# Spreading Q and dO into the padded tile on VectorE, and turning more middle units in pairs by DMA

## The chip, the cores and the metric

The kernel runs on one core of one Trainium2 chip. The metric is the device time of one execution in microseconds (us); the time shown for a kernel is the median of its runs.

## What is computed

The reference is forward and backward of a gated mix of two branches over 2048 tokens of width 512. Branch A is attention with 32 heads of 16 and a sliding causal window of 256 tokens, branch B a gated feed-forward layer of inner width 1376. The kernel returns the output and the gradients of x and of six weights.

```python
def _A_ref(x, wqkv, wo):
    ...
    scores = jnp.einsum("bhqd,bhkd->bhqk", q, k) * (Dh ** -0.5)
    mask = (idx[:, None] - idx[None, :] >= 0) & (idx[:, None] - idx[None, :] < W)
    p = _softmax(jnp.where(mask[None, None], scores, -1e9), axis=-1)
    ...
g = _sigmoid((x * gate_w).sum(-1, keepdims=True))
return g * _A_ref(x, wqkv, wo) + (1 - g) * _B_ref(x, W_gate, W_up, W_down)
...
_out, _vjp = jax.vjp(_f, A_x, A_wqkv, A_wo, B_W_gate, B_W_up, B_W_down, gate_w)
```

## The kernel before

There are three stages: feed-forward with its weight gradients (0 to about 248 us), attention forward and backward (to about 712 us), and the output with the gradient of x (to the end). The change lies in attention.

**Units.** Attention goes over 4 columns c of 8 heads (128 features), in each over 16 query blocks j of 128 tokens, and in each block over up to 3 key blocks kb and 2 halves (every second head, 4 heads). One (c, j, kb, half) is a unit; there are 360, listed at L646 to L660. The role of a unit is "d" (diagonal, kb = j), "m" (middle, kb = j - 1) or "f" (far, kb = j - 2). Half 1 of a block takes its units in the order m, d, f.

**One unit.** TensorE makes the scores ST (L671) and, from dO and V, dPT (L698). ScalarE takes the exponential of ST into Pu (L684). For "d" and "f" GpSimd masks it (L686, L689). VectorE multiplies it by dPT into Pd (`gradp`, L703). Three units later (LAG) TensorE uses Pu and Pd in the row sums BA (L712, L714); at a block's end ScalarE copies BA to SBUF (L718), and small operations on VectorE and GpSimd make from it the rows rq.

**PSUM.** ST, dPT, the projections (`pp`) and the gradient pieces (`wps`) share the tag M with 4 banks. A bank of ST is free after the exponential, one of dPT after `gradp`.

**Turning.** The gradients of K and V (CD, L533 and L536) need Pu and Pd transposed. `flip` (L723) has two ways. If `u.dma` is set, SyncE issues one transposing DMA (L731); with `u.pair` both halves of a block are turned by one DMA once half 1 is done, else half 0 alone. If it is not set, TensorE does 8 transposes of 128 x 128 (L741) into PSUM, and ScalarE and VectorE by turns copy them out (`evac`, L72 or L74). Before the change "d" units are pairs; "m" units of columns 0 to 2 are pairs for odd j, and for j = 4, 6, 8 in columns 1 and 2; in the other even blocks half 0 goes by DMA, from the tile PPs with one buffer, and half 1 over TensorE. Pairs of "m" lie in PPm with two buffers, pairs of "d" in PPd with three. Far units always go over TensorE.

**Groups and the padded tile.** Four blocks form a group gi = (c, tg) of 512 tokens; there are 16. During a group the planner projects the next one (`project_parts`, L118): Q, dO, a row transpose by DMA (`tr_rows`, L171), K, V, and K and V turned to rows (`tr_kv`). Q and dO land side by side in the tile zT (128 x 2 x 512). ST and dPT handle four heads at once, so they need Q and dO in a padded tile `zt`: four copies of the 512 columns of which copy k holds only partitions 32k to 32k + 31, with zeros elsewhere. `spread` (L512) fills part k. For the first group this is done by small copies in `mm` (L151); for the 15 others by four DMAs from SyncE.

**The order.** It is written by the loop at L877, one step per unit n. Operations planned for later stand in `ev` by step, with their engine's name: "pool" ones come ahead of `gradp`, "dve" ones behind it, "dma" ones at the end of the step. `credit` estimates TensorE's spare time and decides when a projection part (`prq`) or a gradient piece (`bgq`) is taken; a unit that turns over TensorE costs 0.44 (L934). When Q and dO of the next group have been projected (`len(prq) == 4`, L951), the four spreads and `flush` (stores that have gathered) are planned as "dma" at step n + 1; `tr_rows` is the next projection part. All DMAs named here, transposing or plain, are issued by SyncE in this order.

Of the kernel before, what the change touches and what calls it, by code (L numbers as in the profile page):

```python
# [22 lines left out]
def kernel(  # L23
# [20 lines left out]
    nc = tc.nc  # L44
# [11 lines left out]
    DC = D // P  # L56
# [48 lines left out]
    ZB = 2  # L105
    wq = ctx.enter_context(tc.tile_pool(name="wq", bufs=1))
    zt = [wq.tile([P, 2, NP, TPG, P], BF, tag=f"z{i}", name=f"z{i}") for i in range(ZB)]
# [4 lines left out]
    if True:  # L112
        HH = HG // 2
        proj = {}
        groups = [(c, tg) for c in range(DC) for tg in range(NTG)]
# [74 lines left out]
    with ExitStack() as p1, tc.manual_schedule():  # L190
# [148 lines left out]
        for fc in range(FC):  # L339
            for tg in range(NTG):  # L340
                k = Step()
# [97 lines left out]
        for n in range(N1 + 8):  # L439
# [35 lines left out]
            t = n - DA0  # L475
# [18 lines left out]
            z = n - DA0 - NT - 2  # L494
# [6 lines left out]
    if True:  # L501
# [9 lines left out]
        pools["now"] = (ps, "M", 4, psr, "TR")  # L511
        def spread(gi, k):  # L512
            rows = slice(32 * k, 32 * k + 32)
            nc.sync.dma_start(zt[gi % ZB][rows, :, k, :, :].rearrange("p w t q -> p w (t q)"),
                              proj[groups[gi]]["z"][rows, :, :])

        P2 = {}
        RQ = {}
# [128 lines left out]
        for c in range(DC):  # L647
            for j in range(NT):
                kbs = [k for k in (j - 1, j, j - 2) if k >= 0]
                for half in range(2):  # L650
                    order = kbs if half or len(kbs) < 3 else [kbs[0], kbs[2], kbs[1]]
                    for ki, kb in enumerate(order):
                        u = Unit()
                        u.c, u.j, u.kb, u.half = c, j, kb, half
                        u.first = ki == 0 and half == 0
                        u.last = ki == len(kbs) - 1 and half == 1
                        u.role = ("d", "m", "f")[j - kb]
                        u.pair = u.role == "d" or (u.role == "m" and c < DC - 1 and (j % 2 == 1 or (c > 0 and j in (4, 6, 8))))
                        u.dma = u.pair or (u.role == "m" and half == 0 and (c < DC - 1 or j < 10))
                        units.append(u)  # L660
        NU = len(units)
# [177 lines left out]
        with tc.manual_schedule():  # L839
            ev = {}  # L840
# [6 lines left out]
            n = 0  # L847
# [6 lines left out]
            def background():  # L854
                f, more = bgq.pop(0)
                store = f()
                if store is not None:
                    copies.append(store)
                    if len(copies) > 2 or gi + 2 >= len(groups):
                        ev.setdefault(n + 2, []).append(("dma", flush))  # L860
                return more
# [15 lines left out]
            while n <= NU + LAG or ev or cdq or bgq:  # L877
                now = ev.pop(n, [])
                u = units[n] if n < NU else None
                if u is not None:  # L880
                    gi = u.c * NTG + u.j // TPG
# [30 lines left out]
                w = units[n - LAG] if LAG <= n < NU + LAG else None  # L912
# [24 lines left out]
                if n >= NU:  # L937
                    if bgq:
                        held = background()
                    elif n > NU + 1:  # L940
                        for _ in range(2):
                            if len(S2["grads"]) > DC:
                                S2["grads"].pop(0)()
                elif held and credit > 0.3:
                    held = background()
                    credit -= 0.65
                elif prq and not held and ((credit > 0.4 and n > fed + 1) or due - n <= len(prq)):
                    fed = n
                    credit -= (0.44, 0.86, 0.86, 0.1, 0.86, 0.86)[len(prq) - 1]
                    prq.pop(0)()  # L950
                    if len(prq) == 4:  # L951
                        for k in range(NP):
                            ev.setdefault(n + 1, []).append(("dma", lambda gi=gi, k=k: spread(gi + 1, k)))
                        ev.setdefault(n + 1, []).append(("dma", flush))
                    if not prq:
                        late += plan.get(gi + 1, [])
                elif bgq and len(prq) <= 2 and credit > 0.3:
                    held = background()
                    credit -= 0.65
# [25 lines left out]
    with ExitStack() as p56:  # L985
        x_r5 = x_r

        with ExitStack() as p6:
# [20 lines left out]
            for g in range(NG):  # L1009
# [3 lines left out]
                for tl in range(GT):  # L1013
                    t = g * GT + tl
# [108 lines left out]
```

## Time and profile before

| | |
|---|---|
| median of 3 runs | 918.95 us (917.79 to 922.31) |
| profiled execution | 917.72 us, its span 916.0 us |
| p2m<-PPm, p2m<-PPs, p2d<-PPd: transposing DMAs (L731) | 36, 18, 62 |
| their median time from issue to landing (PPm, PPs, PPd) | 5.3, 4.4, 5.4 us |
| z<-zT (L514), plain DMAs of 64 KB | 60, 2.8 us to landing |
| TensorE transposes at L741 | 1184 (148 units of 8) |
| copies p2m<-pt: ScalarE, VectorE | 23 of 1.012 us, 13 of 0.683 us |
| `gradp` (L703), PPd, Pd, PPm | 682, 678, 671 ns each |

The profile is one execution on the chip. PE is TensorE, PEld its weight loads, DVE VectorE, ACT ScalarE, POOL GpSimd, SP SyncE; SPq is SyncE's queue of DMA issues. Tiles are named without numbers, so p2m<-PPm is a transpose of any PPm tile. In a timeline a row has the start, the duration, the engine, the line, the operation and the shapes; the bracket at the end tells how long the engine was idle before it and what released it. Matmuls are pipelined, so their durations overlap, and the distance between starts is what one costs. PEclk is the clock that TensorE was granted, in tenths of full speed.

### The profile page before, as it was taken

What the parts mean: (1) busy time and instruction counts of PE and PEld (TensorE: products, weight loads), DVE (VectorE), ACT (ScalarE), POOL (GpSimd) and SP (SyncE); (2) the same over time, 40 slices, a digit from 0 to 9 for tenths busy, and PEclk for the clock granted to TensorE, in tenths of its full rate; (3) what the DMA queues carried; (4) which work ended last, traced back from release to release, by engine and by line L of the source; (5) the groups of instructions that cost most, each with busy time, mean ns of one, the idle gap of its engine ahead of it and who ended that gap; (6) DMA issues with size and microseconds to landing.
All of it is one profiled execution on the core that took longest, in us unless ns stands there. A gap on an engine that the chain in (4) does not pass through costs nothing.

```text
span 916.0 us, 26488 instructions
## 1 busy us (share of the span) xinstructions
PE 899.1 (98%) x10757; PEld 576.2 (63%) x10863; DVE 486.2 (53%) x907; ACT 446.1 (49%) x782; POOL 486.5 (53%) x937
## 2 busy tenths in 40 slices
PE   8999999999999999999999999999999999999998
PEld 5556656556657777667676677777777644444445
DVE  4433344334277777657776677776677222322323
ACT  6422232222368777667776677776688200000111
POOL 4544545445276777767777577775677321111111
PEclk9999999999999999999999999999999999999999
DMA  9998879999699999998999989999999999777741
GB/s 300 194 200 188 192 179 216 221 219 200 159 167 160 170 158 164 178 177 169 178 172 184 186 163 179 179 169 171 186 155 191 251 237 254 183 184 185 184 92 47
DMA packets 490923, 168.07 MB, mean 183 GB/s; under 512 B 414960, under 2 KB 489680, under 8 KB 490800
## 3 DMA queue, kind: packets, MB, share of 16 engines
q1 hardware_dynamic: 470160, 144.46, 85.0%
q10 hardware_dynamic: 19008, 17.31, 6.5%
q0 software_dynamic: 1632, 4.59, 1.4%
q8 instruction: 85, 1.39, 0.6%
q14 instruction: 38, 0.31, 0.1%
HBM read 32.28 MB, written 36.24 MB: 75 GB/s over the span
## 4 chain that ended last, share of the span: by engine, by line
PE 72%; DMA 7%; SPq 6%; POOL 4%; ACT 4%; issue 4%; DVE 2%; ACTq 0%; POOLq 0%; DVEq 0%
PE ST L671 8%; PE dPT L698 7%; PE dxps L1048 6%; PE pt L741 6%; PE wps L403 5%; PE wps L626 4%; PE CD L533 4%; PE BA L712 4%; PE dxps L1052 4%; PE pp L128 3%; PE bps L1021 3%; PE CD L536 2%; PE dhps L354 2%; PE BA L714 2%; PE gps L354 2%
## 5 line engine op out<-in xcount | busy, mean ns | idle before, releaser
L671 PE MATMUL ST<-z,K 128*128 128x512 bf16 x360 | 135.9, 378 | 2.8 <-ACT PPs L684 0.8
L698 PE MATMUL dPT<-z,V 128*128 128x512 bf16 x360 | 136.0, 378 | 1.0 <-DVE Pd L703 0.2
L686 POOL TENSOR_SCALAR_AFFINE_SELECT PPd<-PPd 128x512 bf16<-128x512 bf16 x124 | 78.7, 634 | 109.5 <-ACT PPd L684 108.9
L703 DVE TENSOR_TENSOR Pd<-Pu,dPT 128x512 bf16<-128x512 bf16 x148 | 99.9, 678 | 65.6 <-POOL Pu L689 58.1
L368 POOL TENSOR_TENSOR hT<-rg,upm 128x512 bf16<-128x512 bf16 x44 | 51.9, 1179 | 115.1 <-DVE upm L366 94.8
L684 ACT ACTIVATE Pu<-ST 128x512 bf16<-128x512 f32 x148 | 88.8, 600 | 36.6 <-PE ST L671 35.6
L403 PE MATMUL wps<-dgu_r,x_r 128*128 128x256 bf16 (+1 forms) x704 | 103.9, 270 | 1.2 <-DVE wst L74 0.2
L703 DVE TENSOR_TENSOR PPd<-PPd,dPT 128x512 bf16<-128x512 bf16 x124 | 84.5, 682 | 23.9 <-POOL PPd L686 22.2
L403 PEld LDWEIGHTS <-x_r 128*128 128x128 bf16 x704 | 68.3, 98 | 31.1 <-issue 0.9
L684 ACT ACTIVATE PPd<-ST 128x512 bf16<-128x512 f32 x124 | 74.8, 603 | 20.2 <-PE ST L671 19.9
L1028 ACT COPY a_sb<-aps 128x512 f32<-128x512 f32 x16 | 9.4, 586 | 151.7 <-issue 137.9
L689 POOL TENSOR_SCALAR_AFFINE_SELECT Pu<-Pu 128x512 bf16<-128x512 bf16 x112 | 71.8, 641 | 20.3 <-ACT Pu L684 19.8
L366 DVE SCALAR_TENSOR_TENSOR upm<-rg,ups 128x512 bf16<-128x512 bf16 x44 | 30.1, 685 | 80.1 <-PE ups L354 38.9
L360 ACT ACTIVATE rg<-gps 128x512 bf16<-128x512 f32 x44 | 26.3, 598 | 87.8 <-PE gps L354 43.3
L405 PE MATMUL dps<-db_r,h_r 128*128 128x512 bf16 x159 | 60.3, 379 | 0.0
L378 POOL TENSOR_TENSOR dgu<-dh_sb,rg 128x512 bf16<-128x512 bf16 x44 | 56.9, 1293 | 5.1 <-ACT dh_sb L374 5.1
L741 PE MATMUL pt<-ident,Pd 128*128 128x128 bf16 x592 | 57.2, 219 | 0.0
L741 PE MATMUL pt<-ident,Pu 128*128 128x128 bf16 x592 | 56.7, 217 | 0.0
L1034 POOL DMA_DIRECT2D out_dram<-o_sb x16 | 8.7, 541 | 85.9 <-DVE o_sb L1032 79.5
L72 ACT COPY p<-pt 128x1024 bf16<-128x1024 bf16 x51 | 52.2, 1024 | 2.1
L684 ACT ACTIVATE PPm<-ST 128x512 bf16<-128x512 f32 x70 | 42.3, 604 | 17.2 <-PE ST L671 16.9
L626 PE MATMUL wps<-rows_st,x_r 128*128 128x384 bf16 x256 | 50.3, 325 | 0.0
(196 smaller groups left out, 2370.1 us busy)
## 6 DMA issues: line engine op xcount, KB each, us to landing
dqkvo_d<-rows_st SPq DMA_DIRECT2D x15, 512.0 KB, 3.5
hT_d<-hT ACTq DMA_DIRECT2D x44, 128.0 KB, 2.5
dgT_d<-dgu ACTq DMA_DIRECT2D x44, 128.0 KB, 2.8
duT_d<-dgu ACTq DMA_DIRECT2D x44, 128.0 KB, 3.0
duT_g<-duT_d SPq DMA_DIRECT2D x8, 640.0 KB, 5.6
gt<-hT_d SPq DMA_DIRECT2D x7, 640.0 KB, 5.9
dgT_g<-dgT_d SPq DMA_DIRECT2D x7, 640.0 KB, 4.9
z<-zT SPq DMA_DIRECT2D x60, 64.0 KB, 2.8
```

The lines of the kernel that those rows point to most:

```text
L378: nc.gpsimd.tensor_tensor(out=k.duT, in0=dh_sb[:], in1=k.rg[:], op=ALU.mult)
L403: nc.tensor.matmul(acc["w"][:, c, 0:2 * nw], lhsT=x_r[:, t, c * P:(c + 1) * P], rhs=k.dgu_r[:, :, i, s0:P], start=(go_ and c % 2 == 0), st ...
L405: nc.tensor.matmul(acc["d"][:], lhsT=k.h_r[:, i, :], rhs=db_r[:, t, :], start=go_, stop=no_)
L626: nc.tensor.matmul(wps[:], lhsT=x_r[:, t, part * P:(part + 1) * P], rhs=sts[c][:, t, 0:3, :], start=first and t == t0, stop=last and t == ...
L671: nc.tensor.matmul(ST[:], lhsT=KTt[:, ksl], rhs=z[:, 0, :, jl, :], start=True, stop=True)
L684: nc.scalar.activation(u.Pu[:], ST[:], ACT.Exp)
L686: nc.gpsimd.affine_select(out=u.Pu[:], in_=u.Pu[:], compare_op=ALU.is_ge, fill=0.0, base=0, pattern=[[0, HH], [1, P]], channel_multiplier=-1)
L689: nc.gpsimd.affine_select(out=u.Pu[:], in_=u.Pu[:], compare_op=ALU.is_ge, fill=0.0, base=-1, pattern=[[0, HH], [-1, P]], channel_multiplier=1)
L698: nc.tensor.matmul(u.dPT[:], lhsT=VTt[:, ksl], rhs=z[:, 1, :, jl, :], start=True, stop=True)
L703: nc.vector.tensor_tensor(out=u.Pd[:], in0=u.Pu[:], in1=u.dPT[:], op=ALU.mult)
L741: nc.tensor.transpose(pt[:, a, hh, :], src[:, hh, :], ident[:])
L1048: nc.tensor.matmul(to, lhsT=src[:, fc, lsl], rhs=W6[(wt, fc)][:, cols], start=(fc == 0 and wt == "Wg"), stop=False)
```

## The change

It has three lines. The spreads of the 15 later groups become VectorE copies of 32 partitions by 2 x 512 elements, and are planned one per step at n + 1 to n + 4 behind `gradp`, not all four at the end of step n + 1. "m" units of even blocks from j = 4 on are turned as pairs in all of the first three columns: new are 4, 6, 8, 10, 12, 14 in column 0 and 10, 12, 14 in columns 1 and 2. The last column's units, and block 2, stay as they are.

```diff
         def spread(gi, k):
             rows = slice(32 * k, 32 * k + 32)
-            nc.sync.dma_start(zt[gi % ZB][rows, :, k, :, :].rearrange("p w t q -> p w (t q)"),
-                              proj[groups[gi]]["z"][rows, :, :])
+            nc.vector.tensor_copy(zt[gi % ZB][rows, :, k, :, :].rearrange("p w t q -> p w (t q)"),
+                                  proj[groups[gi]]["z"][rows, :, :])
...
-                        u.pair = u.role == "d" or (u.role == "m" and c < DC - 1 and (j % 2 == 1 or (c > 0 and j in (4, 6, 8))))
+                        u.pair = u.role == "d" or (u.role == "m" and c < DC - 1 and (j % 2 == 1 or j > 2))
                         u.dma = u.pair or (u.role == "m" and half == 0 and (c < DC - 1 or j < 10))
...
                     if len(prq) == 4:
                         for k in range(NP):
-                            ev.setdefault(n + 1, []).append(("dma", lambda gi=gi, k=k: spread(gi + 1, k)))
+                            ev.setdefault(n + 1 + k, []).append(("dve", lambda gi=gi, k=k: spread(gi + 1, k)))
                         ev.setdefault(n + 1, []).append(("dma", flush))
```

## The prediction, made before the changed kernel ran

> **What bounds the kernel now.** I read four views: busy shares with the slices, TensorE's waits, the chain of waits through attention (248 to 712 us, where all of the change lies), and the timelines of VectorE and SyncE there.
>
> ```profile
> span 916.0 us, 26488 instructions
> PE 899.1 (98%) x10757; PEld 576.2 (63%) x10863; DVE 486.2 (53%) x907; ACT 446.1 (49%) x782; POOL 486.5 (53%) x937
> PEclk9999999999999999999999999999999999999999
> ```
>
> The reader should see that TensorE is busy for 98% of the span at its full clock. In the table by stage it is busy 434.99 of the 440 us from 272 to 712, VectorE 313.14, ScalarE 325.15, GpSimd 312.55; so attention is paced by TensorE's own instructions, and an instruction taken off it is time. As a second test I added up TensorE's issue costs between the starts of all ST and dPT matmuls (0.215 us for 512 columns, 0.057 for a transpose, 0.025 for a small BA or CD matmul, all read from distances between starts). They fill all but 9.4 of 462 us; 3.9 of the 9.4 lie before 272 us, and the largest single stall, 0.97, is at 444.7. The chain of waits shows what made that one, and what a turn on TensorE costs:
>
> ```profile
> 440.81 0.46 PE pt L741 x8
> 442.11 4.14 DMA p2m<-PPs
> 446.33 0.60 ACT PPs L684
> ```
>
> Eight transposes are 0.46 us of TensorE. The exponential of block 12 (column 1) waited for PPs, which has a single buffer, until the transpose of block 10 had landed. The queue was late. SyncE's timeline says why (start, duration, queue):
>
> ```profile
> 421.71 3.45 SPq L514 DMA_DIRECT2D z<-zT  x4
> 425.20 1.28 SPq L619 DMA_DIRECT2D out_dram<-ws  x2
> 426.53 0.62 SPq L554 DMA_DIRECT2D dqkvo_d<-rows_st  x1
> 427.25 1.70 SPq L173 DMA_TRANSPOSE rows<-zT  x1
> 429.05 3.52 SPq L731 DMA_TRANSPOSE p2m<-PPm  x1
> 442.11 1.24 SPq L731 DMA_TRANSPOSE p2m<-PPs  x1
> ```
>
> From 421.7 to 452 SyncE issues almost without a gap. I laid each transpose beside the ST of the unit at which the code asks for it: the one at 429.05 is 6.0 us late, the one at 442.11 8.3.
>
> **TensorE.** The condition adds twelve (column, block) pairs: 4 to 14 in column 0 (six), 10, 12, 14 in columns 1 and 2. In each, half 1 leaves the TensorE path: 8 transposes, 0.46 us. Sum 12 x 0.46 = **-5.5 us**, all on the bound engine. Their 12 copies out of PSUM (ScalarE 1.012, VectorE 0.683 us, alternating) go too: -6 us and -4 us off engines with slack, counted as nothing.
>
> **The stall at 444.7.** PPs is used by those blocks no more: **-1.0 us**. Next late is PPm with its two buffers: block j waits for the transpose of j-2, which is now asked for 7 units (8.1 to 9.3 us) earlier and needs 5.3 to land (median of p2m<-PPm), so it may be 2.8 to 4 us late. Today those of block 8 are 6.0 and 5.7 late (columns 1 and 2). With the four spreads (3.1 to 3.5 us) out of the queue ahead of them I expect 2.5 to 3: just inside. I take 0; if the cover fails, some 2.4 us at each of two places.
>
> **SyncE and the DMA engines.** 60 issues of z<-zT go, 3.0 to 3.6 us for each four: -47 us of SyncE over 15 groups. A transpose of one half becomes one of two, median 1.5 to 2.6 us of issue: +13. When behind (429 to 453) the queue takes 16 halves in 23.9 us, 1.49 each, so the 12 halves are 18 us of its time at most. The queue gets shorter in every group: two or three halves (3 to 4.5 us) against 3.1 to 3.5 of spreads and the stop they make. Nothing gained or lost but what stands above. That `flush` and the row transposes (L173) stand 3 us further forward helps the same queue. The planner sees 12 units without a TensorE turn, each 0.44 more credit, and takes projections and gradient pieces a unit or so earlier: the same work, counted at nothing; if it falls badly, a stall of the 0.1 to 0.3 us that stand at the ends of some groups now.
>
> **VectorE.** It gets 60 copies of 32 x 1024 bf16, one in each of four consecutive units, behind that unit's gradp (L703). A copy waits for dO's evacuation on its own engine, so for nothing new, and the next group's first ST comes 15 us or more later. No row has this size. The nearest is the first group's own spread (line, engine, count, ns min/median/max):
>
> ```profile
> L74 DVE COPY z<-zT x6: 280/284/290, 225.5 to 231.9; 32x512 bf16<-32x512 bf16 x6
> L161 DVE TENSOR_SCALAR V<-VT,par x32: 346/353/517, 240.3 to 667.2; 128x512 bf16<-128x512 bf16 x32
> ```
>
> Twice the elements cost at least 284 ns (all fixed) and at most 568 (all per element); between the ends I take the middle, 0.43. The four copies at 225.50 take 1.18 us, 0.295 apart: they don't overlap, while two L703 start 0.60 apart at 0.68 each. So I add 0.10 for the overlap lost on both sides: **0.53 us per copy**, between 0.35 (0.43 with the usual overlap) and 0.68 (0.57 without). [...]
>
> What does VectorE do there? One group:
>
> ```profile
> 303.53 0.69 DVE L74 CAST zT<-pp 128x512 bf16<-128x512 f32 x1 [0.65 <-PE pt L741]
> 304.14 0.68 DVE L703 TENSOR_TENSOR PPd<-PPd,dPT 128x512 bf16<-128x512 bf16 x1
> 304.73 0.20 DVE L758 RECIPROCAL rinv<-BAs 128x8 f32<-128x8 f32 x1
> 304.85 0.64 DVE L703 TENSOR_TENSOR Pd<-Pu,dPT 128x512 bf16<-128x512 bf16 x1
> 305.40 0.69 DVE L74 COPY p<-pt 128x1024 bf16<-128x1024 bf16 x1
> 306.02 0.69 DVE L703 TENSOR_TENSOR PPd<-PPd,dPT 128x512 bf16<-128x512 bf16 x1
> 307.62 0.69 DVE L703 TENSOR_TENSOR Pd<-Pu,dPT 128x512 bf16<-128x512 bf16 x1 [0.92 <-PE dPT L698]
> 309.35 0.61 DVE L161 TENSOR_SCALAR K<-KT,par 128x512 bf16<-128x512 bf16 x2 [1.04 <-ACT KT L72]
> ```
>
> A late gradp hurts only when TensorE wants its PSUM bank back. The four M banks go round in order of release, so I could read each slack: the gradp at 304.85 ends 0.90 us before its bank is written again, the one at 307.62 0.64, the one at 306.02 gives its bank to the K projection, 1.4 later. With copies behind the gradps at 304.14, 304.85, 306.02 and 307.62 the delays are 0.53 (under 0.90), 1.06 (under 1.4), 1.59 less the idle 0.92 = 0.67 (over 0.64 by 0.03), then 1.20 less 1.04 idle. So this group loses nothing to speak of; groups at a column's start, with their short blocks, lose 0.4 to 0.5. Pushed so through all 15 groups: 0 us at 0.35 per copy, **1.9 at 0.53**, 7.8 at 0.68.
>
> **Sum.** -5.5 - 1.0 + 1.9 = -4.6. The profiled execution took 917.7 (span 916.0 and 1.7 around it), so 913.1. The median shown, 918.95, is 1.2 higher, because one of the three runs took 922.31 while the lowest is 917.79; for a median I add most of that: **914.0 us**.
>
> **Rivals.**
> - *VectorE costs nothing* (copies at 0.35, or the idle time falls better): -6.5 to -7, 911 to 912. For: VectorE idles 29% from 272 to 712. Against: the spacing of copies. 0.18.
> - *The gain is eaten.* Copies at 0.68 give -6.5 + 7.8 = +1.3 on 917.7, 919; or PPm is late at block 10 of columns 1 and 2, each 2.4: -4.6 + 4.8 = 918. This includes that the change doesn't do what it says: that the DMA engines, not SyncE's issues, made the queue late, so that removing small spreads frees nothing. For: TensorE's stall at 444.7 came from this queue. Against: the queue was on time again at 407 and 415, after three blocks of full pairs. 0.27, between 915.5 and 923.5.
> - *Slower: copies blocked by GpSimd.* In the first stage a VectorE tensor_scalar between SBUF tiles took 342/789/2976 ns (da_t, L329), beside GpSimd's long products. If the copies wait as its median did, 0.45 more, each costs 0.98, and the same push gives 22.9 us: 917.7 - 6.5 + 22.9 = 934. From 0.66 per copy on there is no gain left. Against: K and V (L161), the same kind of instruction in attention with GpSimd busy for 71%, take 353 at the median and 517 at most. [...] 0.13.
>
> **Numbers.** The forecast (912.5 to 915.5) has 0.42. A measurement here tells about 0.5% (4.6 us) from no change: faster is below 914.4, slower above 923.5. Faster: 0.18 and some three quarters of 0.42: 0.50. Slower: 0.13 and 0.02 from the end of the second rival: 0.15. Same: 0.35. The range is 909.5 to 922.0: it leaves out the blocked copies and the edges of the others.
>
> **What would show it.** Right: 1088 transposes at L741 instead of 1184; z<-zT as a VectorE row near 0.43 us; no stall near the old 444.7; transposes behind a group's start at most 3 us late. Wrong: that row above 0.6; TensorE waiting for L703 in the four units behind dO's projection; ScalarE's PPm waiting for p2m<-PPm; TensorE's idle time in attention above 11 us. I would be most wrong if GpSimd's selects (L686, L689) became longer too, since the push leaves them as they are.

## The result and the profile after

The changed kernel takes 927.42 us (median of 4 runs, 926.99 to 927.63) against 918.66 for the kernel before beside it: a ratio of 1.0084, 95% interval 1.0062 to 1.0106. It is slower by 8 us, where 4.6 us less was forecast. The profiled execution took 927.52. The head of its page (busy us, share of the span, instructions):

```profile
span 925.8 us, 26308 instructions
PE 906.1 (98%) x10767; PEld 572.3 (62%) x10767; DVE 517.0 (56%) x961; ACT 439.6 (47%) x776; POOL 493.0 (53%) x937
```

TensorE's busy time went up by 7 us although 96 transposes were taken away. This line can't tell work from waiting. In the profile a matmul of 512 columns lasts 0.38 us while the next one starts 0.215 us later, so the end of one matmul covers a short wait of the next. Also, 106 matmuls are missing from the records of the kernel before (10757, beside 10863 weight loads; the changed kernel has 10767 of each). The sum of issue costs from the prediction can tell them apart. From the first ST to the last dPT it gives:

- before: 462.3 us, of which 452.9 issue cost and 9.4 stalls
- after: 472.3 us, of which 447.4 issue cost and 24.9 stalls

The 5.5 us of transposes did come off. Stalls of 15.5 us came on; the sum, +10.0, is the lengthening of attention, and the stages ahead of it and behind it kept their lengths within 0.3 us. In the changed kernel the stalls lie in columns 0 and 2 (7.9 and 6.7 us), while columns 1 and 3 have 3.3 and 3.1.

The new copies and the multiplications of K and V (count, ns min/median/max), and K's before the change:

```profile
L514 DVE COPY z<-zT x60: 366/456/720, 253.8 to 672.3; 32x1024 bf16<-32x1024 bf16 x60
L161 DVE TENSOR_SCALAR K<-KT,par x32: 309/485/760, 239.6 to 674.4; 128x512 bf16<-128x512 bf16 x32
L161 DVE TENSOR_SCALAR V<-VT,par x32: 341/352/583, 240.1 to 676.3; 128x512 bf16<-128x512 bf16 x32
```

```profile
L161 DVE TENSOR_SCALAR K<-KT,par x32: 340/350/500, 239.8 to 664.2; 128x512 bf16<-128x512 bf16 x32
```

The copy's median is near the 0.43 of the prediction, but it reaches 0.72, and K's multiplication went from 0.35 to 0.485 (V's stayed at 0.35). VectorE's timeline in the group that answers to the one shown before, and GpSimd's beside it:

```profile
305.57 0.68 DVE L703 TENSOR_TENSOR PPd<-PPd,dPT 128x512 bf16<-128x512 bf16 x1
306.16 0.20 DVE L758 RECIPROCAL rinv<-BAs 128x8 f32<-128x8 f32 x1
306.28 0.37 DVE L514 COPY z<-zT 32x1024 bf16<-32x1024 bf16 x1
...
308.45 0.69 DVE L703 TENSOR_TENSOR PPd<-PPd,dPT 128x512 bf16<-128x512 bf16 x1
309.17 0.68 DVE L514 COPY z<-zT 32x1024 bf16<-32x1024 bf16 x1
309.87 0.69 DVE L703 TENSOR_TENSOR Pd<-Pu,dPT 128x512 bf16<-128x512 bf16 x1
310.59 0.65 DVE L514 COPY z<-zT 32x1024 bf16<-32x1024 bf16 x1
311.26 1.03 DVE L161 TENSOR_SCALAR K<-KT,par 128x512 bf16<-128x512 bf16 x2
```

```profile
309.16 0.40 POOL L767 TENSOR_TENSOR rq<-rows,rinv 128x128 bf16<-128x128 bf16 x1
309.52 0.59 POOL L769 TENSOR_TENSOR rows_st<-BAs,rinv 128x128 bf16<-128x128 f32 x1
310.54 0.41 POOL L773 TENSOR_TENSOR BAs<-BAs 128x128 f32<-128x128 f32 x1
```

The first copy meets an idle GpSimd and takes 0.37. The third and fourth run beside GpSimd's small products and take 0.68 and 0.65, and the product at 309.52 takes 0.59, where the longest at that line before was 0.456:

```profile
L769 POOL TENSOR_TENSOR rows_st<-BAs,rinv x64: 396/407/456, 260.6 to 717.0; 128x128 bf16<-128x128 f32 x64
```

It is so in the other groups too: of the 60 copies, twelve overlap no GpSimd instruction and take 0.37 to 0.42 us, and the forty that lie beside its products for more than half of their time take 0.57 at the median. The 0.92 and 1.04 us that VectorE idled in this group before are gone; it is busy without a gap to 313.5.

In columns 0 and 2 a second thing shows, at the end of every block from block 2 on. ScalarE at the end of block 9 of column 0, in the changed kernel and, below it, in the kernel before:

```profile
320.23 0.50 ACT L718 COPY BAs<-BA 128x400 f32<-128x400 f32 x1
320.61 1.04 ACT L72 COPY p<-pt 128x1024 bf16<-128x1024 bf16 x1
321.51 0.64 ACT L684 ACTIVATE PPm<-ST 128x512 bf16<-128x512 f32 x1
322.00 0.64 ACT L684 ACTIVATE PPd<-ST 128x512 bf16<-128x512 f32 x1
```

```profile
317.74 0.50 ACT L718 COPY BAs<-BA 128x400 f32<-128x400 f32 x1
318.29 0.60 ACT L684 ACTIVATE Pu<-ST 128x512 bf16<-128x512 f32 x1
```

In the changed kernel the copy of the far unit's half 1 out of PSUM stands between the row sums and the next block's exponentials. The copies out of PSUM take ScalarE and VectorE by turns. Before, even blocks of column 0 made three such copies and odd ones two, so the engine of far half 1 changed at every second block: ScalarE had it in 8 of the 14 blocks of column 0 and in 4 each of columns 1 and 2. Without the middle unit's copy every block makes two, and the turn stands still: ScalarE has far half 1 in all later blocks of columns 0 and 2, VectorE in column 1.

### The profile page after: what moved, and what is told of

It is laid out like the page before. It is cut to its first block, busy times and chain, and to the rows that moved or that the text cites. A ratio compares the mean times of both kernels' runs of the same rounds, so it can differ in the third digit from the quotient of the medians.

```text
span 925.8 us, 26308 instructions
## 1 busy us (share of the span) xinstructions
PE 906.1 (98%) x10767; PEld 572.3 (62%) x10767; DVE 517.0 (56%) x961; ACT 439.6 (47%) x776; POOL 493.0 (53%) x937
## 4 chain that ended last, share of the span: by engine, by line
PE 73%; POOL 8%; DVE 6%; ACT 4%; DMA 3%; issue 3%; SPq 1%; ACTq 0%; DVEq 0%; POOLq 0%
PE dxps L1048 8%; PE wps L403 7%; PE ST L671 6%; PE dPT L698 5%; PE wps L626 5%; PE dxps L1052 4%; PE pt L741 4%; PE bps L1021 4%; PE dps L405 4%; PE dhps L354 3%; PE pp L128 3%; PE gps L354 3%; PE ups L354 3%; PE CD L533 3%; PE BA L712 3%
## 5 line engine op out<-in xcount | busy, mean ns | idle before, releaser
L686 POOL TENSOR_SCALAR_AFFINE_SELECT PPd<-PPd 128x512 bf16<-128x512 bf16 x124 | 79.1, 638 | 115.9 <-ACT PPd L684 115.4
L703 DVE TENSOR_TENSOR Pd<-Pu,dPT 128x512 bf16<-128x512 bf16 x136 | 92.1, 681 | 58.9 <-POOL Pu L689 50.8
L684 ACT ACTIVATE Pu<-ST 128x512 bf16<-128x512 f32 x136 | 81.5, 600 | 46.8 <-PE ST L671 46.6
L703 DVE TENSOR_TENSOR PPd<-PPd,dPT 128x512 bf16<-128x512 bf16 x124 | 84.4, 680 | 16.6 <-POOL PPd L686 15.4
L689 POOL TENSOR_SCALAR_AFFINE_SELECT Pu<-Pu 128x512 bf16<-128x512 bf16 x112 | 72.7, 649 | 17.3 <-ACT Pu L684 16.1
L360 ACT ACTIVATE rg<-gps 128x512 bf16<-128x512 f32 x44 | 26.3, 597 | 86.3 <-PE gps L354 48.9
L405 PE MATMUL dps<-db_r,h_r 128*128 128x512 bf16 x176 | 66.7, 379 | 0.0
L684 ACT ACTIVATE PPm<-ST 128x512 bf16<-128x512 f32 x94 | 56.8, 605 | 20.3 <-PE ST L671 19.4
L703 DVE TENSOR_TENSOR PPm<-PPm,dPT 128x512 bf16<-128x512 bf16 x94 | 63.0, 671 | 4.5 <-POOL PPm L686 1.6
L128 PE MATMUL pp<-x,p 128*128 128x512 bf16 x192 | 49.0, 378 | 4.7 <-DVE PPm L703 2.8
L741 PE MATMUL pt<-ident,Pd 128*128 128x128 bf16 x544 | 52.6, 219 | 0.0
```

The costliest lines, as they stand in the source:

```text
L128: nc.tensor.matmul(pp[:], lhsT=w_p[c][:, cd, which * P:(which + 1) * P], rhs=x_T[tg][:, cd, :], start=(cd == 0), stop=(cd == DC - 1))
L405: nc.tensor.matmul(acc["d"][:], lhsT=k.h_r[:, i, :], rhs=db_r[:, t, :], start=go_, stop=no_)
L684: nc.scalar.activation(u.Pu[:], ST[:], ACT.Exp)
L686: nc.gpsimd.affine_select(out=u.Pu[:], in_=u.Pu[:], compare_op=ALU.is_ge, fill=0.0, base=0, pattern=[[0, HH], [1, P]], channel_multiplier=-1)
L689: nc.gpsimd.affine_select(out=u.Pu[:], in_=u.Pu[:], compare_op=ALU.is_ge, fill=0.0, base=-1, pattern=[[0, HH], [-1, P]], channel_multiplier=1)
L703: nc.vector.tensor_tensor(out=u.Pd[:], in0=u.Pu[:], in1=u.dPT[:], op=ALU.mult)
```

## The experiments

Each run is told by its ratio to the kernel before on the same chip, and by its stalls in attention, found as above in its profiled execution (us; "first" is the first 18 units, then columns 0 to 3). The runs were spread over several chips, on which the kernel before has medians of 917.71 to 919.26 us, so kernels are compared by the ratios rather than by the medians.

| kernel | median us | ratio (95% interval) | first | c 0 | c 1 | c 2 | c 3 | sum |
|---|---|---|---|---|---|---|---|---|
| before | 918.66 | | 3.4 | 1.5 | 1.9 | 1.2 | 1.4 | 9.4 |
| changed | 927.42 | 1.0084 (1.0062, 1.0106) | 3.9 | 7.9 | 3.3 | 6.7 | 3.1 | 24.9 |
| e1 copies alone | 924.34 | 1.0065 (1.0047, 1.0084) | 4.0 | 2.5 | 3.0 | 3.0 | 3.3 | 15.8 |
| e2 pairs alone | 927.96 | 1.0105 (1.0086, 1.0123) | 3.4 | 9.2 | 6.8 | 5.8 | 1.1 | 26.3 |
| e3 changed, other turn | 922.45 | 1.0045 (1.0030, 1.0061) | 3.9 | 2.7 | 6.7 | 3.8 | 3.1 | 20.2 |
| e4 changed, turn fixed | 919.97 | 1.0021 (1.0012, 1.0031) | 3.9 | 2.7 | 3.6 | 4.0 | 3.3 | 17.4 |
| e5 pairs, turn fixed, 3 PPm | 918.73 | 0.9994 (0.9979, 1.0010) | 3.4 | 1.6 | 2.0 | 3.1 | 2.6 | 12.8 |
| e6 pairs, turn fixed | 925.31 | 1.0059 (1.0043, 1.0076) | 3.4 | 6.1 | 7.6 | 5.7 | 1.3 | 24.2 |
| e8 reductions added | 922.97 | 1.0031 (1.0018, 1.0044) | 3.9 | 1.6 | 2.7 | 2.0 | 1.9 | 12.0 |
| e9 e4, copies 3 steps apart | 919.55 | 1.0000 (0.9988, 1.0012) | 4.1 | 3.7 | 3.4 | 3.7 | 2.1 | 17.0 |
| e10 e5, spreads on ScalarE's queue | 921.31 | 1.0033 (1.0021, 1.0045) | 4.4 | 3.0 | 4.3 | 4.2 | 3.8 | 19.6 |
| e11 e9, two copies and two DMAs | 914.37 | 0.9957 (0.9944, 0.9970) | 3.5 | 1.7 | 2.6 | 2.5 | 1.6 | 11.8 |
| e12 before, turn fixed | 916.80 | 0.9988 (0.9973, 1.0002) | 3.4 | 0.5 | 1.9 | 1.7 | 1.3 | 8.9 |
| e13 e6, spreads on ScalarE's queue | 922.19 | 1.0047 (1.0033, 1.0061) | 4.3 | 3.0 | 4.1 | 4.1 | 3.3 | 18.8 |
| e14 copies added | 925.13 | 1.0070 (1.0046, 1.0095) | 3.9 | 2.4 | 3.8 | 3.0 | 3.3 | 16.3 |
| e15 reductions added | 922.88 | 1.0043 (1.0030, 1.0056) | 3.9 | 1.6 | 2.0 | 2.0 | 1.9 | 11.3 |

The first theory was the alternation (B), that is, the turn that stands still; its rivals were the copies by themselves (A) and the queue (C).

**e1, the copies alone.** The changed kernel with the old pairs.

```diff
-                        u.pair = ... (j % 2 == 1 or j > 2))
+                        u.pair = ... (j % 2 == 1 or (c > 0 and j in (4, 6, 8))))
```

> Only the spreads move to VectorE; the pairs stay as in the kernel before. The changed kernel waits on TensorE 24.9 us in attention against 9.4 before, mostly in columns 0 and 2. Theory A (the copies): VectorE's 60 copies, some stretched from 0.37 to 0.7 us beside GpSimd's products, cost all of the 15.5 us by themselves, so this run gives about 919 + 15 = 934. Theory B (the alternation): taking away one copy out of PSUM in every even block leaves two per block, so that in columns 0 and 2 the far unit's half 1 is always copied by ScalarE, right behind the row sums, and only there the copies hurt; alone they cost little more than in column 1 of the changed kernel, about 1 us per column: 919 to 924.

Measured +6.0 us by the ratio, 6.4 more of stalls, spread over all columns (1.0 to 1.9 each). A asked for 15, B for at most 5: the copies cost more than B allowed and much less than all of it, and columns 0 and 2 are not singled out.

**e2, the pairs alone.** The kernel before with the new condition; the spreads stay DMAs.

> Only the pairs are added; the spreads stay DMAs. Theory A: without the copies nothing costs, TensorE's 5.5 us and the stall of 1 us are won: 912 to 913. Theory B: the alternation is the same as in the changed kernel, so columns 0 and 2 lose about 1 us in each of their groups, 917 to 921. Theory C (the queue): the spreads are still in it, PPm is late at block 10 of columns 1 and 2, some 2.4 us each: ScalarE's PPm shows waits for p2m<-PPm, 915 to 918.

Measured +9.6 us, slower than any theory had it. ScalarE's waits, and TensorE's behind them (us in total, times, longest):

```profile
ACT PPm L684 <- DMA p2m<-PPm: 11.8, 7, 2.9
```

```profile
PE ST L671 <- ACT PPm L684: 6.1, 5, 1.6
PE dPT L698 <- ACT PPm L684: 3.5, 3, 2.3
```

C holds, and larger than priced: exponentials waited 11.8 us for PPm to be turned, and 9.6 of it reached TensorE. Behind three of these waits there was a second loss: the clock that TensorE was granted fell to half for 3.4 us each (from 317.2, 348.0 and 470.8 us). In one of these stretches (busy us and count of PE, PEld, DVE, ACT and POOL, then the granted clock, the DMA share and GB/s):

```profile
317.30:320.60 3.30, 3.30 (x45) 2.20 (x42) 1.49 (x3) 2.90 (x6) 1.64 (x3) 0.50 1.15 212
```

The clock is 0.50, and matmuls of 512 columns start 0.43 us apart, not 0.215. Of e2's stalls in the table 3.8 us are such slower matmuls (2.6 in column 0, 1.2 in column 1). The profiles of the kernel before and of the changed kernel show no such stretch in attention. In the changed kernel the exponentials wait for PPm for 0.4 us in all. Taking the spreads out of SyncE's queue made PPm come in time, as the prediction said it would.

**e3 and e4, the turn of the copies.** Both are the changed kernel; e3 starts the turn at the other engine, e4 fixes it for far units of columns 0 to 2.

```diff
-        copier = {"i": 0}
+        copier = {"i": 1}
```
```diff
-            eng = ("act", "dve")[copier["i"] % 2]
-            copier["i"] += 1
+            if u.c < DC - 1 and u.role == "f":
+                eng = ("act", "dve")[u.half]
+            else:
+                eng = ("act", "dve")[copier["i"] % 2]
+                copier["i"] += 1
```

> The changed kernel, with the alternation of the copies out of PSUM started at VectorE instead of ScalarE: columns 0 and 2 then have far half 1 on VectorE, column 1 on ScalarE. Nothing else differs. Theory B: columns 0 and 2 lose their stalls (about 9 us), column 1 gets some 4: 921 to 924, and the stalls move to 365 to 480 us. Theory A: the time stays at 926 to 928.

> The changed kernel, with far units of columns 0 to 2 copied out of PSUM by ScalarE for half 0 and by VectorE for half 1 always, so that all three columns are as column 1 is in the changed kernel. Theory B: the stalls of columns 0 and 2 go, 917 to 920, and with the shorter TensorE work perhaps level with the kernel before. Theory A: 926 to 928.

Both came out as B had it. In e3 the stalls change places: column 0 from 7.9 to 2.7, column 2 from 6.7 to 3.8, column 1 from 3.3 to 6.7. In e4 all three are low, and the stalls are 7.5 us less than in the changed kernel (17.4 against 24.9). The medians differ by as much; by the ratios, 1.0021 against 1.0084, it is 5.8 us. ScalarE at the same place in e4:

```profile
318.53 0.50 ACT L718 COPY BAs<-BA 128x400 f32<-128x400 f32 x1
319.09 0.60 ACT L684 ACTIVATE PPm<-ST 128x512 bf16<-128x512 f32 x1
320.00 0.60 ACT L684 ACTIVATE PPd<-ST 128x512 bf16<-128x512 f32 x1 [0.32 <-PE ST L671]
320.71 1.01 ACT L72 COPY p<-pt 128x1024 bf16<-128x1024 bf16 x1
```

The exponentials follow the row sums at once, the second even waits for TensorE, and the 1 us copy (now half 0) stands where a unit has passed.

**e5 and e6, the pairs with the fixed turn.** e6 is e2 with e4's edit. e5 also gives PPm three buffers.

```diff
-                    if u.pair or (u.c == DC - 1 and u.j % 3 > 0):
-                        kind = ...
-                        nh, tag, bufs = 2, f"PP{kind}", {"d": 3, "m": 2}[kind]
-                    else:
-                        nh, tag, bufs = 1, "PPs", 1
+                    kind = ...
+                    nh, tag, bufs = 2, f"PP{kind}", 3
```

> The pairs without the copies, far half 1 always copied by VectorE in columns 0 to 2, PPm as it was (two buffers). The pairs alone gave 928, with 26.3 us of stalls: 9.2, 6.8 and 5.8 in columns 0, 1, 2, of which ScalarE's waits of PPm for p2m<-PPm make up about 9.6 on TensorE. If both causes stand and add up, the alternation's part (some 5 us in columns 0 and 2) goes and the queue's part stays: 921 to 924, with the waits for p2m<-PPm still near 12 us. If the alternation does it all, 913; if the queue does it all, 928.

> The pairs without the copies, far half 1 always copied by VectorE in columns 0 to 2, and PPm with three buffers (PPs is given up for it, and P2f has three buffers in place of four, for want of SBUF). If the pairs lose only to the alternation and to PPm's two buffers, nothing of that is left here: TensorE's 5.5 us and the stall of 1 us are won, 911 to 914, faster than both kernels. If the DMA engines themselves cannot carry the added halves, PPd or the CD matmuls wait instead: 916 to 922. A fourth of P2f's buffers may be missed, which would show as ScalarE or VectorE copies p<-pt waiting for CD.

e6 keeps PPm's waits (13.1 us on ScalarE) and has 2.1 us of stalls less than e2. TensorE had half its clock here too, for 13.7 us in all, and 4.8 us of e6's stalls are slower matmuls. Without these, e6 has 3.1 us less than e2: 1.7 and 1.4 in columns 0 and 2, 0.3 in column 1. So without the copies the standing turn costs some 3 us. Its 7.5 us in the changed kernel are not a price of its own; they come where the copies are there too. In e5 PPm waits no more. Stalls are 12.8, but the time is level with the kernel before: SyncE's queue is still late, PPd waits now (5.1 us on ScalarE), and the last CD matmuls wait 2.7 us for p2d<-PPd, behind the stretch that the table covers. The profiled execution had full clock throughout; in seven of e5's ten runs the mean granted clock was 0.996 to 0.998, so its whole time may hold half-clock stretches that this profile doesn't show. The expected 911 to 914 was missed.

**e8, e14, e15, VectorE's time or the conflict with GpSimd.** All keep the spreads as DMAs and add one VectorE operation per step at the copies' places; what it writes is used by nothing.

```diff
+        def extra(gi, k):
+            rows = slice(32 * k, 32 * k + 32)
+            scr = pjA.tile([P, 1], F32, tag="scr", name="scr")
+            nc.vector.reduce_max(scr[rows, :], proj[groups[gi]]["z"][rows, 0, 0:288], axis=AX.X)
...
+                            ev.setdefault(n + 1 + k, []).append(("dve", lambda gi=gi, k=k: extra(gi + 1, k)))
```

> The kernel before, spreads still by DMA, plus 60 added VectorE reductions of 32 x 288 elements at the places of the copies (one per step, n + 1 to n + 4); their results are used by nothing, so the kernel does more work than the reference needs. Each should last near 0.45 us, as the copies do at the median, but reads a single stream and writes one number. The copies alone cost 6.6 us. If it is VectorE's time that they cost, this costs as much: 923 to 926. If it is the copies getting in the way of GpSimd's products (and these stretching them), this costs 1 to 3: 919 to 921.

> The kernel before with its spreads by DMA, and 60 added VectorE copies of 32 x 1024 elements from zT into a tile that nothing reads, at the places of the changed kernel's copies (more work than the reference needs). P2f has three buffers in place of four to make room. If the copies conflict with GpSimd's products, they last 0.37 to 0.72 us as in the changed kernel and cost what the copies alone cost, 5 to 7 us: 923 to 926. If the cost came with the missing DMAs, this costs no more than the reductions, 3 us: 920 to 922.

> The same with 60 reductions of 32 x 288 elements in place of the copies, P2f again with three buffers: 920 to 923, the reductions at 0.39 to 0.45 us. The difference to the run with copies is what the copies cost beyond VectorE's time: 3 us if they conflict with GpSimd, 0 to 1 if not.

The added operation in e14 and in e15:

```profile
L520 DVE COPY scr<-zT x60: 366/476/720, 252.7 to 668.2; 32x1024 bf16<-32x1024 bf16 x60
```

```profile
L520 DVE TENSOR_REDUCE scr<-zT x60: 392/444/450, 256.7 to 667.4; 32x1 f32<-32x288 bf16 x60
```

Reductions of nearly the same median are never stretched and add 1.9 us of stalls (e8: 2.6). Copies are stretched just as in the changed kernel and add 6.9, with the DMAs still in place. So the copies' extra cost did not come with the missing DMAs: about 2 us is VectorE's time, and 4 to 5 us come with the stretching. That GpSimd causes it is read from where the stretched copies lie; no run keeps the copies and takes GpSimd's products away. The sizes rest on one profiled execution of each kernel. The whole times say less (e14 925.1, e15 922.9, intervals that overlap); in the profiles, e8 and e15 also lost some 3 us ahead of attention (first ST at 252.0 and 251.4, 247.4 to 250.1 in the other kernels), where their code is that of the kernel before. Why was not tried.

**e9 and e11, placing and halving the copies.** e9 is e4 with the copies at n + 1, n + 4, n + 7, n + 10; e11 is e9 with parts 2 and 3 on SyncE's DMAs again.

```diff
-            nc.vector.tensor_copy(zt...[rows, :, k, :, :]..., proj[groups[gi]]["z"][rows, :, :])
+            copy = nc.vector.tensor_copy if k < 2 else nc.sync.dma_start
+            copy(zt...[rows, :, k, :, :]..., proj[groups[gi]]["z"][rows, :, :])
```

> The changed kernel with far half 1 on VectorE in columns 0 to 2 (920.0), and the four copies three steps apart (n + 1, n + 4, n + 7, n + 10) in place of one per step. If it is the bunching of the copies in the steps in which Q, dO, K and V are evacuated, most of the remaining 8 us of added stalls go: 914 to 917. If each copy costs its own time wherever it stands, 919 to 921.

> The kernel with the copies three steps apart (919.6; far half 1 on VectorE), but only parts 0 and 1 are copied by VectorE, at n + 1 and n + 4, and parts 2 and 3 go by SyncE's DMAs at n + 1 as before the change. If copies and queue each cost in proportion, half of the copies' 7.6 us of added stalls goes and the queue stays short enough for PPm: 915 to 917. If two spreads already make PPm late, ScalarE waits for p2m<-PPm again: 919 to 922.

Spacing moved little (stalls 17.4 to 17.0, ratio 1.0021 to 1.0000): spaced out, fifteen copies fall beside GpSimd's selects (L686, L689) alone and take 0.66 us at the median, and the mean copy lasts 0.55 instead of 0.48. Halving did: 914.37 us, ratio 0.9957, faster than both kernels. Two spreads left in the queue make PPm wait 3.4 us on ScalarE, 1.9 of it on TensorE. The rest of its stalls, 9.9, is near the 9.4 of the kernel before, so two copies per group cost little here.

**e10, e12, e13, controls.** In e10 (from e5) and e13 (from e6) ScalarE's queue issues the spreads' DMAs; e12 is the kernel before with the fixed turn.

```diff
-            nc.sync.dma_start(zt...
+            nc.scalar.dma_start(zt...
...
-                            ev.setdefault(n + 1, []).append(("dma", ... spread(gi + 1, k)))
+                            ev.setdefault(n + 1 + k, []).append(("dma", ... spread(gi + 1, k)))
```

> The pairs with three PPm buffers and far half 1 on VectorE (that kernel: 918.7, level with the kernel before, its span 916.0), and the spreads still DMAs, but issued from ScalarE's queue, one per step at n + 1 to n + 4. SyncE then loses its 47 us of spread issues without VectorE getting any copy. If the rest of that kernel's stalls (1.7, 1.1 and 2.7 us behind p2d<-PPd, at the starts of columns 2 and 3 and at the end) came from SyncE's queue, they go: 911 to 915, faster than both kernels. If the DMA engines are what is full, the issues' place makes no difference: 917 to 920. The issues take ScalarE some 0.4 us each, which could cost 1 to 3 us of late exponentials.

> The kernel before with far half 1 of columns 0 to 2 always copied by VectorE and half 0 by ScalarE; no pairs, no copies. It is the control for the fixed copier: its eight stalls of 0.27 us behind row sums and far copies on ScalarE should go, and VectorE's far copies in some blocks stand beside the middle unit's: 917 to 920, no more than 2 us from the kernel before. If it is several us faster, the fix is a gain of its own and not the repair of what the change did.

> As the run with the spreads on ScalarE's queue, but with PPm's two buffers, PPs and P2f's four as in the changed kernel. With the spreads out of SyncE's queue the two buffers were enough in the changed kernel (0.4 us of waits). If SyncE's issues are what made PPm late: 911 to 916. If it is the DMA engines, PPm waits as in the pairs alone (13 us): 923 to 926.

ScalarE's wait for PPm in e13:

```profile
ACT PPm L684 <- DMA p2m<-PPm: 0.9, 2, 0.6
```

Against 13.1 in e6, with the same bytes moved. So the bytes did not make PPm late; SyncE's issues did. (e13 also issues the four in four steps and e6 in one; this was not tried apart.) But no time was won, and stalls are 18.8 (e13) and 19.6 (e10): 60 issues of 0.6 us now stand in ScalarE's order. In e13 some 25 exponentials whose scores were ready came behind one, 7.3 us late in all. e12 is level with the kernel before (0.9988, interval to 1.0002); the fixed turn repairs what the change did and is hardly a gain of its own.

## Why the prediction was wrong, step by step

Two terms of the sum failed: the 12 copies out of PSUM, which it put at nothing, and the VectorE copies, which it put too low. The others held.

- **TensorE, -5.5 us: right.** Issue cost went from 452.9 to 447.4.
- **The stall at 444.7, -1.0 us: right.** Column 1 has no such stall after.
- **SyncE and the queue: right in what it gives, not in how late.** For block 8 of columns 1 and 2 the PPm transposes start 5.1 and 3.9 us late, where 2.5 to 3 was expected, and other transposes are up to 7 us late. Still, PPm waits only 0.4 us in all. With the spreads left in the queue it waits 11.8 (e2), and e13 shows that the issues matter and not the bytes. The price of failing cover was too low: 2.4 us at two places were forecast; 9.6 on TensorE were measured, and 3.8 more at half clock.
- **The 12 copies out of PSUM, "engines with slack, counted as nothing": wrong, 7.5 us by the stalls, 5.8 by the ratios.** They were counted as work and are also places in a turn. Without them the turn stood still in columns 0 and 2, with ScalarE's 1 us copy ahead of the next block's exponentials (e3, e4). Only together with the VectorE copies is it this dear (e6 against e2: 3).
- **VectorE, 1.9 us: the size failed.** The push of delays through the idle time was good for VectorE's own time: reductions of that length cost 1.9 to 2.6. So was 0.53 us for three of four copies where no GpSimd instruction overlaps them: parts 1 to 3 take 0.42 there, with gaps of 0.03 on both sides where two L703 overlap by 0.08, which makes 0.56. Part 0 takes 0.37 and overlaps its neighbours by 0.08 too, which makes 0.29. But the sum put the stretching beside GpSimd at nothing. With it the mean copy lasts 0.51; counted in the same way, parts 1 to 3 make 0.67 on the mean, close to the 0.68 for which the same push gave 7.8, part 0 makes 0.35, and all four 0.59. The copies alone cost 6.0 to 6.4, 4 to 5 of it with the stretching.
- **The rivals.** "Blocked by GpSimd" had the right sign, and 0.13; the copies of 0.57 us at the median that lie beside GpSimd's products agree with it. It was put low because K and V took 353 ns at the median; with the copies K's median is 485, and V's is unchanged. At 0.98 us per copy it was priced too high: the copies' mean is near 0.5. The selects, which the prediction named as its greatest doubt, became hardly longer (from 0.634 to 0.638 and from 0.641 to 0.649 us on the mean).

The terms don't close to the last us. e4 has 8.0 us more stalls than the kernel before, though the copies alone bring 6.4 and one stall of 1.0 went: 2.6 remain. With TensorE's work 5.5 us shorter the other engines have less slack, which might do it; no run shows it apart.

## What to carry to other kernels

When a change takes an operation out of a round-robin, look which engine each later operation gets, and what stands behind it there. VectorE, idle 29% of the time from 272 to 712 us in the kernel before, was no free place for 60 short copies: beside GpSimd's products they took 0.57 us at the median, alone 0.37 to 0.42. Here the fastest run moved half of the spreads, with the turn fixed, and left half where they were (914.4 us). And read a busy share of 98% together with issue costs: here it stood for 9.4 us of stalls in attention as well as for 24.9.

## What the runs showed of the hardware

- A VectorE copy of 32 x 1024 bf16 took 0.37 to 0.42 us where no GpSimd instruction overlapped it, and 0.57 at the median beside GpSimd's products for more than half of its time; the longest, 0.72, lies beside a memset and a product (changed kernel). The products at L769 went from 0.41 at the median to as much as 0.59. A reduction of 32 x 288 in the same places stayed at 0.39 to 0.45 (e15). 60 copies added 6.9 us of stalls (e14), 60 reductions 1.9 (e15) and 2.6 (e8).
- SyncE's issue of a DMA of 64 KB took 0.60 us at the median (kernel before). With these issues in SyncE's queue, exponentials waited 13.1 us for the transposes of PPm (e6); with the same DMAs from ScalarE's queue, one per step, 0.9 us (e13). There they took 0.6 us each of ScalarE's queue.
- In attention, behind six waits of TensorE of 1.6 to 3.3 us (three each in e2 and e6), its granted clock fell to 0.50 for 3.4 us, once for 6.8. Not every long wait did this: behind one of 2.7 us in e5 (at 721.1) the clock stayed full.
